# Blocks of 64 queries for the score maxima, and three elementwise jobs given to other engines

## The chip, the cores and the metric

One program runs on one core of a Trainium2 chip. The metric is device time in microseconds (us) of one execution; lower is better. The core's engines each work through their own instructions in order and meet through semaphores. They are called here as the profile calls them: TensorE is PE (its weight loads are PEld), VectorE is DVE, ScalarE is ACT, GpSimd is POOL, and SyncE is SP, whose work is to issue DMAs.

## The reference

Two results are computed from separate inputs and laid side by side. The first is causal attention with a sliding window; the second is a long convolution whose taps come from a state space model.

```python
# A: 2048 positions, width 576, 32 heads of 18, window 256
q, k, v = heads(x @ wqkv)
scores = einsum("bhqd,bhkd->bhqk", q, k) * 18 ** -0.5
mask = (i - j >= 0) & (i - j < 256)
p = softmax(where(mask, scores, -1e9))
a = concat_heads(p @ v) @ wo
# B: 2048 positions, 576 channels, 128 states
K = real(sum_n C * exp(dt * A * l) * dt * B)     # (576, 2048)
b = causal_conv(u, K) + u * Dskip                # by FFT of length 4096
out = concatenate([a, b], axis=-1)
```

All inputs and the output are fp32. The kernel keeps that accuracy where it uses 16 bit operands by splitting a number into a high and a low fp16 part.

## The kernel before, in words

The first 470 us project x to q, k and v (stored to memory in fp16, with a high and a low part) and build the taps of the convolution. Two transform steps of the convolution then run (the second, `s1_k`, ends near 515 us; its matmuls are L465 and its evacuations L132 on ScalarE and L134 on VectorE). After that comes the stage to which the change belongs, `attention`, from about 515 us to the end. Its order is written out by hand: what each engine's queue holds, and in which order, is what these loops issue.

**Units and items.** Attention is cut into 16 units: eight groups of four heads, for each half of the 2048 queries. A unit has 1024 queries of four heads, and six items (two chunks of 512 queries, three banks of key blocks each). For item n of 96 the loop interleaves several generators by their progress (`merge` always steps the one that is least advanced; of equals the first in the list). In list order they are: the scores of item n; a share of `gmax` for a later unit; the values of item n-2; a share of the convolution `conv`; and late in the loop parts of the output projection `wo_first` and `wo_part`.

- `scores` has two halves. Each issues the score matmuls (L676) into one of two buffers `ST`, then one exponential on ScalarE (L678, 128 x 1024), which writes `P`. At the end the masks of the diagonal blocks run on GpSimd (L687).
- `values` multiplies `P` by the values of the heads (L699); after a chunk ScalarE copies the sum out (L707).
- `gmax` finds for each query the largest score in its window, which is what the exponential subtracts. It runs one to three units ahead. Its unit begins at the fourth item (k = 3), right after the unit before it has been transposed and closed (L648, L650), so that its first step is issued behind the first half of that item's scores. The step copies q of the four heads into `qb`, a block diagonal operand, with two instructions on VectorE (L632, one for each half of the partitions). Then come 32 steps, one for a block of 32 queries: two matmuls (L640) of 64 columns each (two heads x 32 queries), stacked in one PSUM tile of the pool `ring`, and one fused add-and-maximum over 288 keys on VectorE (L643, followed in the trace by a read of its accumulator). The additive bias hides keys outside of the window. There is one `qb`; the pool `ring` has three buffers, which `conv`, `norm` and the output projection use too.
- `conv` runs in frequency space: matmuls L504, copies X on ScalarE (L527), products on VectorE (L530, L531, L534, L535), differences and sums on GpSimd (L539, L540), the inverse L511 with its copies on ScalarE (L512). From about 1000 us its last part runs in 16 rounds: load h (SP queue, L555) and u (GpSimd's queue, L559), multiply u by Dskip on GpSimd (L573), a matmul (L577), an add on VectorE (L579), and four stores through the SP queue (L123 is the helper that issues postponed DMAs).
- `norm` scales a finished unit: L735, L738 and L748 on VectorE, the high part of the quotient on ScalarE (L749), the low part on VectorE (L751), the matmul that spreads the denominators (L747), and four stores on GpSimd's queue (L755).

The maxima come back as a row of the operand `Q` through four small DMAs of the SP queue (`Q<-m`, issued by L123 one item after the transpose).

Of the kernel before, what the change touches and what calls it, by code (L numbers as in the profile page):

```python
# [10 lines left out]
F32 = mybir.dt.float32  # L11
F16 = mybir.dt.float16
BF = mybir.dt.bfloat16
I32 = mybir.dt.int32
AF = mybir.ActivationFunctionType
OP = mybir.AluOpType
# [22 lines left out]
def constants():  # L39
    c = {}  # L40
    tau = 2 * np.pi
    l1, l2, f1, f2 = np.arange(32), np.arange(64), np.arange(32), np.arange(64)
    ph = -tau * np.outer(l1, f1 + 0.25) / 32
    w1 = np.zeros((128, 2, 128))
    for s in range(4):
        w1[s * 32:s * 32 + 32, 0, s * 32:s * 32 + 32] = np.cos(ph)
        w1[s * 32:s * 32 + 32, 1, s * 32:s * 32 + 32] = np.sin(ph)
    w2 = np.zeros((128, 32, 128))
    i1 = np.zeros((128, 32, 128))
    for f in range(32):  # L50
        ph = -tau * np.outer(l2, f + 0.25 + 32 * f2) / 2048
        co, si = np.cos(ph), np.sin(ph)
        w2[0:64, f, 0:64], w2[64:128, f, 0:64] = co, -si
        w2[0:64, f, 64:128], w2[64:128, f, 64:128] = si, co
        i1[0:64, f, 0:64], i1[64:128, f, 0:64] = co.T, si.T
        i1[0:64, f, 64:128], i1[64:128, f, 64:128] = -si.T, co.T
    ph = tau * np.outer(f1 + 0.25, l1) / 32
    i2 = np.zeros((128, 64))
    for p in range(2):
        i2[p * 64:p * 64 + 32, p * 32:p * 32 + 32] = np.cos(ph) / 2048  # L60
        i2[p * 64 + 32:p * 64 + 64, p * 32:p * 32 + 32] = -np.sin(ph) / 2048
    mult = {"c_cm": np.arange(64), "c_ct": np.arange(32) + 0.5, "c_ca": np.r_[64 * np.arange(8), 512 * np.arange(4)],
            "c_cp": np.r_[np.zeros(8), np.full(4, 31.5)]}
    for nm, v in mult.items():
        t = np.zeros((3, GC, GC, len(v)))
        for g in range(GC):
            t[:, g, g] = v
        c[nm] = t.reshape(96, GC, len(v))
    bias = np.zeros((128, 2, 32))
    for p in range(128):  # L70
        bias[p, 0, :p % 32 + 1] = -1e30
        bias[p, 1, p % 32 + 1:] = -1e30
    c["c_w1"], c["c_w2"], c["c_i1"], c["c_i2"] = w1, w2, i1, i2
    c["c_id"], c["c_bias"] = np.eye(128), bias
    row = np.zeros((32, 32))
    row[18] = 1.0
    c["c_heads"] = np.concatenate([np.kron(np.eye(4), np.ones((32, 32))), np.tile(np.eye(32), (4, 1)),
                                   np.kron(np.eye(4), row)], axis=1)
    return {k: np.ascontiguousarray(v.astype(ml_dtypes.bfloat16 if k in mult else np.float32)) for k, v in c.items()}
# [27 lines left out]
class Kernel:  # L107
# [376 lines left out]
    def conv(self):  # L484
        nc, a, tt = self.nc, self.a, self.nc.vector.tensor_tensor
        fs, fy = self.p["fs"], self.p["fy"]

        def load(fp):
            t = {}
            for nm, src in (("w2", a["c_w2"]), ("i1", a["c_i1"])):  # L490
                t[nm] = fs.tile([128, 2, 128], F32, name=nm)
                nc.sync.dma_start(t[nm], src[:, 2 * fp:2 * fp + 2])
            for nm, g in (("tx", self.gx), ("tk", self.gk)):
                t[nm] = fs.tile([128, 4, 2, 144], F32, name=nm)
                nc.sync.dma_start(t[nm], g.rearrange("a l (s f) j -> (a l) s f j", s=4)[:, :, 2 * fp:2 * fp + 2, :])
            return t
# [20 lines left out]
        nx = load(0)  # L517
        last = None
        for fp in range(16):
            cu = nx  # L520
            ho = fs.tile([128, 2, D], F32, name="ho")
            for hs in range(2):
# [22 lines left out]
                if hs == 0 and fp < 15:  # L545
                    nx = load(fp + 1)
# [17 lines left out]
        nx = [loadh(0), loadh(1)]  # L564
        for _ in range(5):
            yield
        for qd in range(16):
            if qd < 14:
                nx.append(loadh(qd + 2))
            hp, ut = nx[qd]  # L570
            y = fy.tile([128, D], F32, name="t2")
            for e in range(qd + (qd > 0), min(qd + 2, 16)):
                nc.gpsimd.tensor_tensor(nx[e][1], nx[e][1], self.dsk, op=OP.mult)  # L573
            for hf in range(2):
                ps = ring()
                for k in range(2):
                    nc.tensor.matmul(ps[64 * k:64 * k + 64], self.i2, hp[:, k, hf * 288:hf * 288 + 288],  # L577
                                     start=True, stop=True)
                tt(y[:, hf * 288:hf * 288 + 288], ps, ut[:, hf * 288:hf * 288 + 288], op=OP.add)  # L579
                yield  # L580
            for k in range(4):
                self.after(1, nc.sync.dma_start, outv[4 * qd + k], y[32 * k:32 * k + 32])


    def att_setup(self):
        nc, a, ap = self.nc, self.a, self.p["att"]
        self.ident = ap.tile([128, 128], F32, name="ident")
        nc.sync.dma_start(self.ident, a["c_id"])
        self.bias = ap.tile([128, 288], F32, name="bias")
        nc.vector.memset(self.bias, 0.0)  # L590
        for e in range(2):
            nc.sync.dma_start(self.bias[:, 256 * e:256 * e + 32], a["c_bias"][:, e])
        self.qb = ap.tile([128, 2, 32, 64], F16, name="qb")
        nc.gpsimd.memset(self.qb, 0.0)
        self.sets = []
        for b in range(3):
            d = {"Q": ap.tile([128, 2, HQ], F16, name="Q%d" % b), "K": ap.tile([128, 2, HK], F16, name="K%d" % b)}
            nc.vector.memset(d["Q"], 0.0)
            for h in (0, 64):
                nc.vector.memset(d["K"][h:h + 32], 0.0)  # L600
                nc.vector.memset(d["K"][h + 32:h + 64], -32768.0)
            self.sets.append(d)
        self.od = self.p["dram"].tile([2, D, L], F16, name="od")
        hd = ap.tile([128, 288], F32, name="heads")
        nc.sync.dma_start(hd, a["c_heads"])
        self.same, self.pick, self.sums = hd[:, 0:128], hd[:, 128:160], hd[:, 160:288]
# [20 lines left out]
    def gmax(self, i):  # L627

        nc, (hf, g), d = self.nc, divmod(i, 8), self.sets[i % 3]
        m = self.p["m"].tile([128, 32], F32, name="m")  # L630
        for u in range(2):
            nc.vector.tensor_copy(self.qb[64 * u:64 * u + 54, :, :, 32 * u:32 * u + 32],  # L632
                                  d["Q"][64 * u:64 * u + 54].rearrange("p b (t q) -> p b t q", q=32))
        yield
        for t in range(32):
            ps = self.p["ring"].tile([128, 512], F32, name="r")
            k0 = 32 * t if hf > 0 or t >= 8 else 256
            n = 32 * t + 288 - k0
            for b in range(2):
                nc.tensor.matmul(ps[64 * b:64 * b + 64, :n], self.qb[:, b, t, :], d["K"][:, b, k0:k0 + n],  # L640
                                 start=True, stop=True, skip_group_check=True)
            jk = self.p["m"].tile([128, 288], F32, name="jk")
            nc.vector.tensor_tensor_reduce(out=jk[:, :n], in0=ps[:, :n], in1=self.bias[:, 288 - n:], scale=1.0,  # L643
                                           scalar=-3e38, op0=OP.add, op1=OP.max, accum_out=m[:, t:t + 1])
            yield
        yield
        mt = self.p["ring"].tile([128, 512], F32, name="r")
        nc.tensor.transpose(mt[:32, :128], m, self.ident)  # L648
        m16 = self.p["m"].tile([32, 128], F16, name="m16")
        nc.vector.tensor_scalar(m16, mt[:32, :128], 2.0 ** -15, None, op0=OP.mult)  # L650
        for j in range(4):
            r = 64 * (j % 2) + 54
            self.after(1, nc.sync.dma_start, d["Q"][r:r + 1, j // 2].rearrange("o (s q) -> o s q", q=32),
                       m16[:, 32 * j:32 * j + 32])
        yield

    BL = [(0, 0, 0, 1), (128, 2, 0, 3), (512, 1, 0, 2), (768, 4, 2, 4), (1024, 3, 1, 4), (1408, 5, 3, 4)]
# [66 lines left out]
    def norm(self, i):  # L724
# [3 lines left out]
        osb = self.osb.pop(i)  # L728
# [11 lines left out]
        if i == 7:  # L740
            h = self.h7[0] = self.p["h7"].tile([128, 2, HQ], F16, name="h7")
        else:
            h = np_.tile([128, 2, HQ], F16, name="oh16")
        for c in range(2):
            cs = slice(c * 512, c * 512 + 512)
            ps = self.p["ring"].tile([128, 512], F32, name="r")
            nc.tensor.matmul(ps, self.same, X[:, 16 * c:16 * c + 16].rearrange("p s q -> p (s q)"), start=True, stop=True)  # L747
            nc.vector.tensor_tensor(osb[:, cs], osb[:, cs], ps, op=OP.mult)  # L748
            nc.scalar.activation(h[:, 0, cs], osb[:, cs], AF.Copy)  # L749
            yield  # L750
            nc.vector.tensor_tensor(h[:, 1, cs], osb[:, cs], h[:, 0, cs], op=OP.subtract)  # L751
        yield
        for j in range(4 if i != 7 else 0):
            f0 = 72 * g + 18 * j
# [258 lines left out]
```

## Time and profile before

| what | us |
|---|---|
| median of 3 runs (lowest, highest) | 1142.4 (1141.99, 1145.32) |
| the profiled execution | 1142.89 |
| its span in the trace | 1141.2 |
| busy: PE, DVE, ACT, POOL | 921.1, 717.9, 624.2, 519.8 |
| mean granted TensorE clock | 0.925 of full speed |

A row of groups reads: line, engine, operation, output <- inputs, shapes, count | busy us, mean ns of one | idle time of that engine just before them, and what ended most of it. A timeline row reads: start, duration, engine, line, operation, tiles, shape, count, and in brackets the idle time before it with what ended it. A row of windows reads: the stretch, its length, then busy us and count for PE, PEld, DVE, ACT and POOL, then the granted TensorE clock, the busy share of the DMA engines and GB/s.

### The profile page before, as it was taken

The page shows a single profiled execution, that of the slowest core. Times are in us where ns is not written, and L with a number is a line of the kernel's source. Part 1 is how long each engine was busy: PE and PEld are TensorE (multiplying, and loading weights), DVE is VectorE, ACT ScalarE, POOL GpSimd, SP SyncE. Part 2 cuts the span into 40 slices and gives each one's busy share as a digit, 9 for nine tenths or more (in the row PEclk, how much of TensorE's full clock was granted, in tenths as well). Part 3 has the DMA queues.
Part 4 walks back from the last instruction along what each step waited for, and adds up shares of the span by engine and source line. Part 5 has one row for each costly group of instructions (what it writes and reads, how often), then busy time and mean ns, then how long its engine had stood idle before and what let it go on. Part 6 is the DMA issues. An engine that isn't in the chain of part 4 may idle for free.

```text
span 1141.2 us, 27005 instructions
## 1 busy us (share of the span) xinstructions
PE 921.1 (81%) x10412; PEld 450.9 (40%) x10412; DVE 717.9 (63%) x1805; ACT 624.2 (55%) x955; POOL 519.8 (46%) x618
## 2 busy tenths in 40 slices
PE   1535879887979789885888889889888999987876
PEld 0313436555545555532333333333333444433325
DVE  2879656866785562266667677787776566563344
ACT  1785778777878842231355555655555455544430
POOL 0014324442644330102355556666756555487860
PEclk9957989898989889998599998999999999999888
DMA  9564423433343325885153464544445334287753
GB/s 272 152 192 138 97 50 90 110 87 84 87 106 65 76 56 124 216 252 159 43 163 117 129 184 115 156 132 125 132 127 153 88 125 142 81 229 214 195 152 129
DMA packets 156186, 152.45 MB, mean 134 GB/s; under 512 B 37001, under 2 KB 134665, under 8 KB 155865
## 3 DMA queue, kind: packets, MB, share of 16 engines
q1 hardware_dynamic: 148488, 132.14, 42.3%
q0 software_dynamic: 6064, 14.60, 4.9%
q10 hardware_dynamic: 1504, 3.99, 1.3%
q8 instruction: 82, 1.34, 0.5%
q14 instruction: 48, 0.39, 0.1%
HBM read 89.27 MB, written 61.01 MB: 132 GB/s over the span
## 4 chain that ended last, share of the span: by engine, by line
PE 50%; DVE 19%; DMA 10%; ACT 9%; issue 7%; SPq 4%; POOL 1%; DVEq 0%; ACTq 0%; POOLq 0%
PE pp L176 8%; PE po L699 7%; PE r L504 6%; PE r L640 6%; PE r L893 4%; PE r L511 4%; PE ST L676 3%; PE pp L465 3%; PE kp L422 3%; PE r L747 3%; PE x L318 2%; DMA gk<-g 2%; DVE tr L362 2%; DMA K<-in_wqkv_dram 2%; DVE jk L643 1%
## 5 line engine op out<-in xcount | busy, mean ns | idle before, releaser
L643 DVE CUSTOM_DVE_ANT_0 jk<-r,bias 128x288 f32<-128x288 f32 (+7 forms) x512 | 206.5, 435 | 121.6 <-PE r L640 118.8
L678 ACT ACTIVATE P<-ST,esc 128x1024 f32<-128x1024 f32 (+1 forms) x192 | 203.3, 1059 | 93.9 <-PE ST L676 89.4
L384 POOL TENSOR_TENSOR m<-A,tr 128x1024 f32<-128x1024 f32 x72 | 149.6, 2099 | 194.1 <-PE kp L422 141.1
L687 POOL TENSOR_SCALAR_AFFINE_SELECT P<-P 128x512 f32<-128x512 f32 x240 | 158.1, 688 | 107.2 <-ACT P L678 105.0
L640 PE MATMUL r<-K,qb 128*64 128x288 f16 (+7 forms) x1024 | 134.9, 301 | 24.6 <-DVE t L531 5.9
L539 POOL TENSOR_TENSOR Y<-t,t 64x288 f32<-64x288 f32 x64 | 54.4, 849 | 149.8 <-DVE t L534 147.9
L699 PE MATMUL po<-P,V 128*32 128x256 f32 (+2 forms) x1408 | 118.8, 410 | 4.3 <-ACT osb L707 2.2
L640 PEld LDWEIGHTS <-qb 128*64 128x64 f16 x1024 | 61.0, 112 | 128.4 <-issue 78.6
L422 PE MATMUL kp<-Q,m 128*32 128x64 f32 x4608 | 87.9, 230 | 27.7 <-DVE Q L405 10.6
L422 PEld LDWEIGHTS kp<-Q,m 128*32 128x32 f32 x4608 | 75.0, 116 | 56.0 <-issue 40.4
L465 PE MATMUL pp<-ut,w 128*128 128x288 f32 x128 | 52.4, 535 | 42.8 <-DMA ut<-in_u_dram 25.8
L676 PE MATMUL ST<-Q,K 64*128 64x384 f16 (+2 forms) x704 | 75.8, 286 | 2.2 <-DMA Q<-m 2.1
L241 DVE SCALAR_TENSOR_TENSOR qst<-pp,qst 128x512 f16<-128x512 f32 x36 | 24.7, 686 | 64.2 <-ACT qst L240 64.1
L749 ACT ACTIVATE oh<-osb 128x512 f16<-128x512 f32 x28 | 17.6, 630 | 78.9 <-DVE osb L748 78.9
L132 ACT ACTIVATE g<-pp 128x288 f32<-128x288 f32 (+1 forms) x84 | 34.5, 447 | 39.7 <-DMA gk<-g 19.9
L504 PE MATMUL r<-tx,w 128*64 128x288 f32 x256 | 47.0, 448 | 10.8 <-DMA tx<-gx 9.2
L540 POOL TENSOR_TENSOR Y<-t,t 64x288 f32<-64x288 f32 x64 | 53.2, 831 | 3.8
L465 PEld LDWEIGHTS pp<-ut,w 128*128 128x128 f32 x128 | 28.8, 244 | 63.4 <-issue 26.4
L511 PE MATMUL r<-Y,i 128*128 128x288 f32 x128 | 50.7, 480 | 3.7 <-DVE m L643 1.5
L330 ACT ACTIVATE ab<-k 128x512 f32<-128x512 f32 (+1 forms) x54 | 31.9, 591 | 36.5 <-DVE k L329 36.0
L176 PE MATMUL pp<-xh,wh 128*128 128x512 f16 x180 | 47.8, 387 | 1.2 <-DVE xh L233 1.2
L504 PE MATMUL r<-tk,w 128*64 128x288 f32 x256 | 46.4, 443 | 2.8 <-DVE m L643 1.0
(176 smaller groups left out, 1814.3 us busy)
## 6 DMA issues: line engine op xcount, KB each, us to landing
gx<-g SPq DMA_DIRECT2D x32, 288.0 KB
qd<-qst SPq DMA_DIRECT2D x72, 128.0 KB
gk<-g SPq DMA_DIRECT2D x16, 576.0 KB
tx<-gx SPq DMA_DIRECT2D x16, 576.0 KB
tk<-gk SPq DMA_DIRECT2D x16, 576.0 KB
h<-ho SPq DMA_DIRECT2D x16, 576.0 KB
raw<-in_xT_dram SPq DMA_DIRECT2D x16, 512.0 KB
Q<-qd SPq DMA_DIRECT2D x32, 216.0 KB
```

The source lines that it names most:

```text
L176: self.nc.tensor.matmul(ps, u, v, start=(i == 0), stop=(i == len(ops) - 1))
L384: self.nc.gpsimd.tensor_tensor(m, A[:, ch, a0:a0 + 8].unsqueeze(3).to_broadcast(sh), tr[:, ch, part, 0:8].unsqueeze(2).to_broadcast(sh), o ...
L422: nc.tensor.matmul(kp[32 * st:32 * st + 32, c % 2 * JJ2 + j, :], m[:, ch, a0:a0 + 32], Q[:, ch, term % 2, :], start=(term == 0), stop=(ter ...
L465: nc.tensor.matmul(ps, self.w1[:, part, :], src[:, o:o + k], start=True, stop=True)
L504: nc.tensor.matmul(ps[64 * par:64 * par + 64], w2[:, par, 64 * part:64 * part + 64], t[:, 2 * hs:2 * hs + 2, par, :], start=True, stop=True)
L511: nc.tensor.matmul(ps, i1[:, par, :], Y[par], start=True, stop=True)
L640: nc.tensor.matmul(ps[64 * b:64 * b + 64, :n], self.qb[:, b, t, :], d["K"][:, b, k0:k0 + n], start=True, stop=True, skip_group_check=True)
L643: nc.vector.tensor_tensor_reduce(out=jk[:, :n], in0=ps[:, :n], in1=self.bias[:, 288 - n:], scale=1.0, scalar=-3e38, op0=OP.add, op1=OP.max ...
L676: nc.tensor.matmul(ps[:, u, o:o + n], d["K"][h, jp, k0:k0 + 128], d["Q"][h, jp, q0:q0 + n], start=True, stop=True, skip_group_check=True)
L678: nc.scalar.activation(pt[:, 2 * jp:2 * jp + 2, lo:hi], ps[:, :, lo:hi], AF.Exp, scale=self.esc)
L687: nc.gpsimd.affine_select(v, v, pattern=[[0, 4], [sg, 128]], compare_op=OP.is_ge, fill=0.0, base=-1 if far else 0, channel_multiplier=-sg)
L699: nc.tensor.matmul(self.po[32 * j:32 * j + 32, t0 * 128:t1 * 128], V[:, kb * 76 + 19 * j:kb * 76 + 19 * j + 32], pt[:, j, o:o + (t1 - t0) ...
```

## The change

Four things change, all in the attention stage.

1. `gmax` takes 64 queries a step. The operand `qb` holds 16 blocks of 128 columns (two heads x 64 queries) for each of the two head pairs b. A step is one matmul of 128 columns for one b against 320 keys, so there are 16 x 2 = 32 steps a unit as before, each with one matmul where there were two. The add-and-maximum covers 320 columns where it covered 288. The bias is one 128 x 320 constant that is loaded whole. The maxima lie in another order, and the four DMAs that bring them back read 16 partitions of 64 elements each, where they read 32 of 32.
2. The two copies into `qb` are issued on ScalarE, at the same place of the program.
3. The low part of the quotients in `norm` is computed on GpSimd.
4. u times Dskip is computed on VectorE.

```diff
-    bias = np.zeros((128, 2, 32))
+    bias = np.zeros((128, 320))
     for p in range(128):
-        bias[p, 0, :p % 32 + 1] = -1e30
-        bias[p, 1, p % 32 + 1:] = -1e30
+        bias[p, :p % 64 + 1] = -1e30
+        bias[p, 256 + p % 64 + 1:] = -1e30
...
             for e in range(qd + (qd > 0), min(qd + 2, 16)):
-                nc.gpsimd.tensor_tensor(nx[e][1], nx[e][1], self.dsk, op=OP.mult)
+                tt(nx[e][1], nx[e][1], self.dsk, op=OP.mult)
...
-        self.bias = ap.tile([128, 288], F32, name="bias")
-        nc.vector.memset(self.bias, 0.0)
-        for e in range(2):
-            nc.sync.dma_start(self.bias[:, 256 * e:256 * e + 32], a["c_bias"][:, e])
-        self.qb = ap.tile([128, 2, 32, 64], F16, name="qb")
+        self.bias = ap.tile([128, 320], F32, name="bias")
+        nc.sync.dma_start(self.bias, a["c_bias"])
+        self.qb = ap.tile([128, 2, 16, 128], F16, name="qb")
...
         for u in range(2):
-            nc.vector.tensor_copy(self.qb[64 * u:64 * u + 54, :, :, 32 * u:32 * u + 32],
-                                  d["Q"][64 * u:64 * u + 54].rearrange("p b (t q) -> p b t q", q=32))
+            nc.scalar.activation(self.qb[64 * u:64 * u + 54, :, :, 64 * u:64 * u + 64],
+                                 d["Q"][64 * u:64 * u + 54].rearrange("p b (t q) -> p b t q", q=64), AF.Copy)
         yield
-        for t in range(32):
-            ps = self.p["ring"].tile([128, 512], F32, name="r")
-            k0 = 32 * t if hf > 0 or t >= 8 else 256
-            n = 32 * t + 288 - k0
+        for t in range(16):
+            k0 = 64 * t if hf > 0 or t >= 4 else 256
+            n = 64 * t + 320 - k0
             for b in range(2):
-                nc.tensor.matmul(ps[64 * b:64 * b + 64, :n], self.qb[:, b, t, :], d["K"][:, b, k0:k0 + n],
-                                 start=True, stop=True, skip_group_check=True)
-            jk = self.p["m"].tile([128, 288], F32, name="jk")
-            nc.vector.tensor_tensor_reduce(out=jk[:, :n], in0=ps[:, :n], in1=self.bias[:, 288 - n:], scale=1.0,
-                                           scalar=-3e38, op0=OP.add, op1=OP.max, accum_out=m[:, t:t + 1])
-            yield
+                ps = self.p["ring"].tile([128, 512], F32, name="r")[:, :n]
+                nc.tensor.matmul(ps, self.qb[:, b, t, :], d["K"][:, b, k0:k0 + n], start=True, stop=True)
+                jk = self.p["m"].tile([128, 320], F32, name="jk")
+                o = 16 * b + t
+                nc.vector.tensor_tensor_reduce(out=jk[:, :n], in0=ps, in1=self.bias[:, 320 - n:], scale=1.0,
+                                               scalar=-3e38, op0=OP.add, op1=OP.max, accum_out=m[:, o:o + 1])
+                yield
...
-            self.after(1, nc.sync.dma_start, d["Q"][r:r + 1, j // 2].rearrange("o (s q) -> o s q", q=32),
-                       m16[:, 32 * j:32 * j + 32])
+            self.after(1, nc.sync.dma_start, d["Q"][r:r + 1, j // 2].rearrange("o (s q) -> o s q", q=64),
+                       m16[j // 2 * 16:j // 2 * 16 + 16, j % 2 * 64:j % 2 * 64 + 64])
...
-            nc.vector.tensor_tensor(h[:, 1, cs], osb[:, cs], h[:, 0, cs], op=OP.subtract)
+            nc.gpsimd.tensor_tensor(h[:, 1, cs], osb[:, cs], h[:, 0, cs], op=OP.subtract)
```

## The prediction, made before the changed kernel ran

> **What bounds the kernel now.** I read the page's chain of work that ended last first, then windows by stage, then groups with their shapes, then the timeline of single units.
>
> ```profile
> PE 50%; DVE 19%; DMA 10%; ACT 9%; issue 7%; SPq 4%; POOL 1%; DVEq 0%; ACTq 0%; POOLq 0%
> ```
>
> ```profile
> 540.00:1020.00 480.00, 425.01 (x3639) 171.08 (x3638) 325.11 (x1198) 259.59 (x362) 283.51 (x417) 0.96 0.45 130
> 1020.00:1110.00 90.00, 73.48 (x591) 28.19 (x589) 35.15 (x80) 39.06 (x51) 69.84 (x104) 0.89 0.72 197
> ```
>
> The reader sees that in the 480 us where score maxima, scores, values and convolution run together TensorE is busy 89% (425.01 of 480), VectorE 68%, GpSimd 59%, ScalarE 54%. So TensorE's queue sets the pace there: work taken from VectorE pays only where TensorE waits for it, and a new stop of TensorE is paid nearly whole. In the 90 us after 1020 the picture is another: TensorE 82%, GpSimd 78%, and the DMA engines rise from 0.45 to 0.72.
>
> **The copies into qb** (change 2) carry most of the sum. The groups give the price on both engines:
>
> ```profile
> L632 DVE COPY qb<-Q 54x2048 f16<-54x2048 f16 x32 | 25.0, 781 | 0.5
> L264 ACT ACTIVATE al<-nA_re 96x2304 bf16<-96x2304 f32 x1 | 2.1, 2122 | 1.7 <-DVE nA_re L296 1.7
> L294 ACT ACTIVATE dt<-dt 128x576 f32<-128x576 f32 x1 | 0.7, 667 | 0.0
> L428 ACT ACTIVATE K<-kp 128x512 f32<-128x512 f32 x18 | 18.5, 1030 | 7.3 <-PE kp L422 7.3
> ```
>
> ScalarE's two plain rows differ by 1455 ns over 1728 elements: 0.842 ns an element. For 2048 elements that is 2122 - 256 x 0.842 = 1906 ns against VectorE's 781. Two copies take 3.81 us. The dear end is L428, which writes in single scattered elements: 1030 ns for 512, twice the plain price. The new copies write runs of 64, so I take the plain price. Now one unit in the timeline:
>
> ```profile
> 624.74 0.39 PE L676 MATMUL ST<-Q,K 64*128 64x128 f16 x4
> 625.05 1.82 DVE L632 COPY qb<-Q 54x2048 f16<-54x2048 f16 x2
> 625.06 0.64 PE L699 MATMUL po<-P,V 128*32 128x256 f32 x8
> 625.26 1.11 ACT L678 ACTIVATE P<-ST,esc 128x1024 f32<-128x1024 f32 x1 [0.95 <-PE ST L676]
> 625.63 0.71 PE L504 MATMUL r<-tk,w 128*64 128x288 f32 x4
> 626.93 0.25 PE L640 MATMUL r<-K,qb 128*64 128x32 f16 x4 [0.59 <-DVE qb L632]
> 627.11 0.39 PE L676 MATMUL ST<-Q,K 64*128 64x128 f16 x4
> 627.87 0.71 PE L504 MATMUL r<-tk,w 128*64 128x288 f32 x4 [0.37 <-DVE m L643]
> ```
>
> After the first half of the scores TensorE has one step of values (L699) and one of convolution (L504) before the first matmul that reads qb, at 626.93, where it already waits 0.59 us for the copies on VectorE. On VectorE these start beside the exponential. On ScalarE, by the program's order, they stand behind it: it ends at 626.37, the copies at 626.37 + 3.81 = 630.18, and with some 0.06 us to wake TensorE (626.93 less the copies' end at 626.87) the matmul starts at 630.24, which is 3.3 us later. Behind it in TensorE's queue stand the second half of the scores (627.11), for which ScalarE's next exponential waits, and everything else: nothing covers the stop. The first and last of the fourteen units that start at a fourth item:
>
> ```profile
> 564.14 1.11 ACT L678 ACTIVATE P<-ST,esc 128x1024 f32<-128x1024 f32 x1 [3.46 <-PE ST L676]
> 566.25 0.32 PE L640 MATMUL r<-K,qb 128*64 128x32 f16 x4 [0.43 <-DVE qb L632]
> ...
> 1001.58 1.12 ACT L678 ACTIVATE P<-ST,esc 128x1024 f32<-128x1024 f32 x1 [2.08 <-PE ST L676]
> 1003.89 0.44 PE L640 MATMUL r<-K,qb 128*64 128x288 f16 x4
> ```
>
> The same sum gives 2.9 us (565.25 + 3.87 - 566.25) and 2.7 us. The fourteen are 2.9, 3.4, 3.3, 3.7, 2.9, 3.4, 3.7, 3.4, 3.7, 3.7, 2.1, 2.0, 2.0, 2.7: 43 us. The smaller ones at the end have 15 matmuls of the output projection ahead of the block matmul. The unit at item 0 adds 1.0. Gross **+44**. Some comes back, because VectorE is no longer behind when TensorE resumes: bracketed waits such as the 0.37 us at 627.87 add up to about 4 us in the 5 us after the first block matmul of these units: **-4** (0 at least; at most -15, one us a unit).
>
> At the very start ScalarE's first copy stands, in the changed order, before three evacuations of the convolution's last transform:
>
> ```profile
> 478.42 0.43 SPq L620 DMA_DIRECT2D Q<-qd  x1
> 479.98 1.32 ACT L132 ACTIVATE g<-pp 128x384 f32<-128x384 f32 x3 [1.08 <-DMA gk<-g]
> ```
>
> ```profile
> X<-in_u_dram POOLq DMA_DIRECT2D x32, 72.0 KB, 4.2
> ```
>
> A load of u from GpSimd's queue lands 4.2 us after its issue; by that, q is there at 482.5, the copy ends at 484.4, and those evacuations start 4.4 us late. The bracket shows that stage waiting for its stores, so I take **+4** (0 to +6, with the second copy).
>
> **The clock after a stop.** TensorE's granted clock halves after a stretch in which it worked little. Around the unit above:
>
> ```profile
> 622.76:626.17 3.41, 2.85 (x31) 1.12 (x27) 2.60 (x9) 2.46 (x4) 2.10 (x3) 1.00 0.82 271
> 626.17:629.59 3.42, 1.97 (x24) 0.99 (x22) 2.75 (x12) 1.78 (x3) 3.00 (x6) 1.00 1.00 325
> 629.59:633.00 3.41, 3.41 (x18) 1.00 (x20) 0.74 (x7) 1.06 (x2) 3.16 (x5) 0.50 0.12 34
> ```
>
> A stretch with 1.97 us of work in 3.42 (58%) was followed by 3.41 us at half speed, while one with 2.85 was not. A stop of some 3.5 us leaves 1.7 us idle in one of two neighbouring stretches at the least, so nearly every unit will now pay. A half-speed stretch does 1.7 us of full-speed work instead of about 2.9 (85% of 3.41), so it loses 1.2, and with 1.3 stretches a stop 1.5 us. Fourteen stops, most of them hit, give 20; less some 5 us that such stretches cost near copies already: **+15** (0 to +30). The Trainium skill, "TensorE: Matmul & The Clock Gate", Part 1, has the clock fall to half after an idle window of about 3.4 us and rise after a busy one; this trace agrees on the length and on the half, and differs in that 58% of work did not save the clock. By the page's idle window alone this term would be near 0 and the sum 15 us lower.
>
> **The block matmuls** (change 1). L640 goes from 1024 to 512 matmuls, but the two of a step ran side by side:
>
> ```profile
> 993.92 0.29 PE L893 MATMUL r<-woh,h 128*128 128x288 f16 x1
> 994.05 0.28 PE L893 MATMUL r<-wol,h 128*128 128x288 f16 x1
> 994.17 0.28 PE L893 MATMUL r<-woh,h 128*128 128x288 f16 x1
> 994.38 0.44 PE L640 MATMUL r<-K,qb 128*64 128x288 f16 x4
> 994.75 0.39 PE L676 MATMUL ST<-Q,K 64*128 64x256 f16 x4
> ```
>
> Full-width matmuls of 288 columns start 0.12 us apart. Two steps of L640 (four matmuls) take 0.37 us until the next group starts, 0.12 for each and 0.1 for a change of tile shape, which also shows at 994.17 to 994.38 (0.21 where the same shape takes 0.12). So a step costs about 0.123 us now and 0.123 x 320/288 = 0.137 then: 512 x 0.014 = +7 us. Shape changes are lost beside the convolution's L504 (same 128*64 shape now) and saved beside L511, L747 and L893 (128*128); between 540 and 1020 us these are 150 and 114 neighbours, so +3. With TensorE at 89%: **+8** (0 to +15).
>
> **The maxima on VectorE.**
>
> ```profile
> L643 DVE CUSTOM_DVE_ANT_0 jk<-r,bias 128x288 f32<-128x288 f32 x448 | 188.6, 453 | 98.0 <-PE r L640 95.7
> L643 DVE CUSTOM_DVE_ANT_0 jk<-r,bias 128x256 f32<-128x256 f32 x8 | 3.4, 422 | 0.5 <-PE po L699 0.2 <-PE r L640 0.2
> L751 DVE TENSOR_TENSOR oh<-osb,oh 128x512 f16<-128x512 f32 x28 | 23.7, 846 | 0.0
> L573 POOL TENSOR_TENSOR X<-X,dsk 128x576 f32<-128x576 f32 x8 | 11.3, 1413 | 1.0 <-DMA X<-in_u_dram 0.8
> L539 POOL TENSOR_TENSOR Y<-t,t 64x288 f32<-64x288 f32 x64 | 54.4, 849 | 149.8 <-DVE t L534 147.9
> ```
>
> 32 columns more cost 31 ns: 512 x 31 = 16 us of busy time, but VectorE waits 96 us for these matmuls, so most lies in its idle time: **+1** (0 to +16). **The low parts** (change 3): VectorE loses L751, 24 us and 2 us of its other form; it runs ahead of maxima that hand back a ring buffer: **-3** (0 to -15). On GpSimd one costs, between 849 ns for 288 and 1413 for 576 columns, 849 + 224 x 1.96 = 1288 ns: 30 make 39 us, in an engine 59% busy whose masks and differences are needed one step or two items later: **+1** (0 to +5). What hides it is GpSimd's idle 41%; without that it would cost the 39.
>
> **u times D** (change 4) and the last stage. GpSimd loses 16 x 1.413 = 22.6 us there and gains some 7 of low parts. VectorE gains 16 x 0.95 = 15 us (846 ns scaled from 512 to 576 columns), in an engine busy 39% of that stage, though the product for the next round now waits in VectorE's queue for u to land, with adds and the remaining maxima behind it.
>
> ```profile
> PE r L747 <- DVE spread L738: 6.5, 1, 6.5
> DVE t L579 <- DMA out_dram<-t: 20.7, 4, 11.7
> DVE t L579 <- DMA t<-in_u_dram: 6.4, 2, 5.3
> ```
>
> Among the waits between 1000 and 1110 us the store of y's buffer is the long one, which the change leaves as it is, so I take **-3** (-15, all that GpSimd sheds, to +15, all that VectorE gains). The four DMAs that return the maxima (L123, x4 at the transpose's heels) fall into the new stop and land earlier for the scores that need them:
>
> ```profile
> 790.57 5.27 DMA Q<-m
> 1007.88 6.07 DMA Q<-m
> ```
>
> These two waits stand in the chain; 3 us each at most, **-3** (0 to -6). The bias load and the memset that goes are under 1 us: 0.
>
> **The sum:** 44 - 4 + 4 + 15 + 8 + 1 - 3 + 1 - 3 - 3 = +60. The profiled execution took 1142.89 (its span 1141.2 and 1.7 around it), 0.5 above the median of the runs shown, 1142.4. So 1142.4 + 60 = **1202 us**.
>
> **Rivals.** (a) The stop is as told, but the clock holds and VectorE's relief gives more back: without the clock's 15 and with 10 more back, 1177. For it: between 540 and 1020 the clock averages 0.96. Against: the 626.17 window. (b) ScalarE's copies cost L428's price, 1.66 ns an element over the same 181 ns fixed (667 - 576 x 0.842), so 3.58 us each: 15 units x 3.3 more, 1252. Against: L428's scattered single elements. (c) Faster: VectorE, not TensorE, paces the loop through the ring of three buffers, so that all it sheds is gained: 25 of copies and 26 of low parts, less 16 and 15, gives -20, 1122. It decides from the point where ScalarE has finished the copies by the time TensorE has run out of other work, 1.9 us after the first scores in the unit at 624.7; the copies take twice that. Against it too: VectorE sat idle 98 us before L643, waiting for TensorE. (d) Fewer matmuls do save time, because the pairs in truth ran one after another: 512 x 0.123 = 63 us less, 1139. Against: four of them in 0.37 us. (e) Each stop holds the clock down for two stretches more: 14 x 2.4 = 34 more, 1236.
>
> **How the numbers follow.** The forecast 0.52, (a) 0.22, (b) 0.08, (c) 0.08, (d) 0.04, (e) 0.06. The range 1165 to 1232 takes in the first two with the bounds of clock, relief and matmuls, and leaves out the rest. Faster by over 0.3% (3.4 us, about what a measurement tells from no change): (c) and half of (d), 0.10; the same 0.02; slower 0.88.
>
> **What the changed profile would show.** L640 waiting 2 to 4 us for ScalarE's qb once a unit, ScalarE's copies at 1.9 us; half-speed windows after most of them; L640's busy time near 70 us; L643 at 484 ns; GpSimd's low parts at 1.3 us; less GpSimd busy after 1020. The prediction is wrong if ScalarE's copies end before TensorE needs them, if the maxima's matmuls take much less of TensorE, or if the last stage shrinks by tens of us.

## The result, and the profile after

The changed kernel takes **1214.47 us** (median; 1212.33 to 1216.53) against 1142.2 for the kernel before on the same chip: a ratio of **1.064 [1.061, 1.067]**, 72 us slower. The forecast was 1202 in a range of 1165 to 1232. The profiled execution took 1212.54 us, its span 1210.8, with TensorE's granted clock at 0.904 on average (0.925 before).

The page's chain of work that ended last, by engine:

```profile
PE 49%; DVE 17%; ACT 14%; DMA 11%; issue 5%; SPq 2%; POOL 1%; DVEq 0%; ACTq 0%; POOLq 0%
```

ScalarE's share went from 9% to 14%, and 4% of the span, some 48 us, is the one line of the copies. The page's groups for the lines that the change touches (L638 and L641 are L640 and L643 of before; L630 was L632, L749 was L751):

```profile
L641 DVE CUSTOM_DVE_ANT_0 jk<-r,bias 128x320 f32<-128x320 f32 (+4 forms) x512 | 221.8, 466 | 200.9 <-PE r L638 199.0
L638 PE MATMUL r<-K,qb 128*128 128x320 f16 (+4 forms) x512 | 138.7, 316 | 67.2 <-ACT qb L630 47.0
L630 ACT ACTIVATE qb<-Q 54x2048 f16<-54x2048 f16 x32 | 60.9, 1902 | 2.0 <-DVE g L134 1.5
```

TensorE stands idle 67.2 us before the maxima's matmuls, and 47.0 of it ends with ScalarE's copy. VectorE lost work, and now waits 200.9 us, nearly all of it for these matmuls, where it waited 121.6. One unit in the timeline of after, which answers to the unit at 624.74 of before (rows of other work between these are left out, here and in the timelines below):

```profile
638.41 0.39 PE L674 MATMUL ST<-Q,K 64*128 64x128 f16 x4
638.92 1.11 ACT L676 ACTIVATE P<-ST,esc 128x1024 f32<-128x1024 f32 x1 [1.11 <-PE ST L674]
639.30 0.71 PE L504 MATMUL r<-tk,w 128*64 128x288 f32 x4
639.93 3.83 ACT L630 ACTIVATE qb<-Q 54x2048 f16<-54x2048 f16 x2
643.82 0.29 PE L638 MATMUL r<-K,qb 128*128 128x64 f16 x2 [3.81 <-ACT qb L630]
644.04 0.61 PE L674 MATMUL ST<-Q,K 64*128 64x128 f16 x4
```

TensorE's last other work starts at 639.30 and ends at 640.01, ScalarE is through its exponential just then, and the two copies run for 3.83 us with TensorE idle for 3.81 of them. The stop comes between two halves of the scores, as the prediction had it. Windows of one length of the clock's records, over the same unit:

```profile
639.00:642.41 3.41, 1.00 (x12) 0.20 (x4) 0.82 (x2) 3.39 (x3) 2.75 (x5) 1.00 1.06 349
642.41:645.82 3.41, 2.00 (x12) 0.65 (x12) 0.38 (x4) 2.46 (x2) 0.00 (x0) 0.50 0.23 64
645.82:649.23 3.41, 3.35 (x17) 1.14 (x18) 1.61 (x8) 1.11 (x1) 2.66 (x4) 0.50 0.00 0
649.23:652.65 3.42, 3.22 (x34) 1.36 (x32) 2.24 (x11) 2.78 (x5) 3.35 (x6) 1.00 0.00 0
```

A stretch with 1.00 us of TensorE work is followed by one at half speed. That one still holds part of the stop (2.00 of 3.41 busy), so the next is at half speed too; only after a full one does the clock come back. The windows of the stage as a whole:

```profile
540.00:1020.00 480.00, 393.01 (x2740) 134.87 (x2738) 266.46 (x1024) 278.07 (x349) 254.22 (x375) 0.90 0.39 114
515.00:1063.00 548.00, 446.31 (x3098) 156.13 (x3099) 301.99 (x1167) 305.50 (x386) 284.53 (x421) 0.90 0.38 113
1063.00:1180.00 117.00, 94.06 (x713) 35.26 (x711) 55.28 (x129) 52.51 (x65) 70.15 (x124) 0.88 0.67 187
```

In the same 480 us TensorE is busy 82% (393.01) where it was 89%, at a clock of 0.90 where it was 0.96. From 515 us to the last unit's copies it takes 548 us where it took 486 (515 to 1001): 62 of the 70 us between the two spans. The rest to the end is 147 where it was 140, with one more stop in it.

### The profile page after: what moved, and what is told of

Same layout as the page of the kernel before. It is cut to its first block, busy times and chain, and to the rows that moved or that the text cites. A ratio compares the mean times of both kernels' runs of the same rounds, so it can differ in the third digit from the quotient of the medians.

```text
span 1210.8 us, 25609 instructions
## 1 busy us (share of the span) xinstructions
PE 948.1 (78%) x9900; PEld 435.2 (36%) x9900; DVE 698.9 (58%) x1758; ACT 683.9 (56%) x987; POOL 513.9 (42%) x632
## 4 chain that ended last, share of the span: by engine, by line
PE 49%; DVE 17%; ACT 14%; DMA 11%; issue 5%; SPq 2%; POOL 1%; DVEq 0%; ACTq 0%; POOLq 0%
PE pp L176 7%; PE po L697 7%; PE r L504 6%; PE r L638 6%; PE r L891 4%; PE ST L674 4%; ACT qb L630 4%; PE r L511 3%; PE kp L422 3%; PE r L745 3%; PE pp L465 3%; DMA gk<-g 2%; DVE jk L641 2%; PE x L318 2%; DVE tr L362 2%
## 5 line engine op out<-in xcount | busy, mean ns | idle before, releaser
L641 DVE CUSTOM_DVE_ANT_0 jk<-r,bias 128x320 f32<-128x320 f32 (+4 forms) x512 | 221.8, 466 | 200.9 <-PE r L638 199.0
L685 POOL TENSOR_SCALAR_AFFINE_SELECT P<-P 128x512 f32<-128x512 f32 x240 | 146.1, 638 | 155.7 <-ACT P L676 153.8
L638 PE MATMUL r<-K,qb 128*128 128x320 f16 (+4 forms) x512 | 138.7, 316 | 67.2 <-ACT qb L630 47.0
L697 PE MATMUL po<-P,V 128*32 128x256 f32 (+2 forms) x1408 | 124.2, 426 | 4.0 <-ACT osb L705 1.4
L539 POOL TENSOR_TENSOR Y<-t,t 64x288 f32<-64x288 f32 x64 | 53.3, 832 | 167.3 <-DVE t L534 165.4
L638 PEld LDWEIGHTS <-qb 128*128 128x128 f16 x512 | 43.0, 100 | 177.2 <-issue 92.2
L674 PE MATMUL ST<-Q,K 64*128 64x384 f16 (+2 forms) x704 | 79.2, 298 | 3.0 <-DMA Q<-m 3.0
L630 ACT ACTIVATE qb<-Q 54x2048 f16<-54x2048 f16 x32 | 60.9, 1902 | 2.0 <-DVE g L134 1.5
L540 POOL TENSOR_TENSOR Y<-t,t 64x288 f32<-64x288 f32 x64 | 51.2, 800 | 3.8
L504 PE MATMUL r<-tk,w 128*64 128x288 f32 x256 | 49.4, 467 | 1.8 <-DVE t L531 0.7
```

What stands on the lines that cost most here:

```text
L504: nc.tensor.matmul(ps[64 * par:64 * par + 64], w2[:, par, 64 * part:64 * part + 64], t[:, 2 * hs:2 * hs + 2, par, :], start=True, stop=True)
L630: nc.scalar.activation(self.qb[64 * u:64 * u + 54, :, :, 64 * u:64 * u + 64], d["Q"][64 * u:64 * u + 54].rearrange("p b (t q) -> p b t q", ...
L638: nc.tensor.matmul(ps, self.qb[:, b, t, :], d["K"][:, b, k0:k0 + n], start=True, stop=True)
L641: nc.vector.tensor_tensor_reduce(out=jk[:, :n], in0=ps, in1=self.bias[:, 320 - n:], scale=1.0, scalar=-3e38, op0=OP.add, op1=OP.max, accum ...
L674: nc.tensor.matmul(ps[:, u, o:o + n], d["K"][h, jp, k0:k0 + 128], d["Q"][h, jp, q0:q0 + n], start=True, stop=True, skip_group_check=True)
L685: nc.gpsimd.affine_select(v, v, pattern=[[0, 4], [sg, 128]], compare_op=OP.is_ge, fill=0.0, base=-1 if far else 0, channel_multiplier=-sg)
```

## The experiments

Each is the kernel before or the kernel after with one edit. The ratio is to the kernel before on the same chip. "Half-speed time" is what the clock's records after 515 us show at half speed, in windows of 3.41 us of which several can follow each other: 80 us in the trace of before, 151 in that of after. Of the longer edits only the main lines are shown.

### Which part costs: the copies back, and the copies alone

The kernel after with its copies on VectorE again (`a_copies_dve`), and the kernel before with nothing changed but its copies put on ScalarE (`b_copies_act`):

```diff
-            nc.scalar.activation(self.qb[64 * u:64 * u + 54, :, :, 64 * u:64 * u + 64],
+            nc.vector.tensor_copy(self.qb[64 * u:64 * u + 54, :, :, 64 * u:64 * u + 64],
...
-            nc.vector.tensor_copy(self.qb[64 * u:64 * u + 54, :, :, 32 * u:32 * u + 32],
+            nc.scalar.activation(self.qb[64 * u:64 * u + 54, :, :, 32 * u:32 * u + 32],
```

> The changed kernel with one part undone: the two copies into qb are back on VectorE, everything else as changed. Theory S (the stop of TensorE for ScalarE's copies, and the half-speed stretches after it, are nearly the whole loss): 1142 to 1152 us, no wait of 2 us or more before the first block matmul of a unit, and half-speed time after 515 us back from 151 to about 80 us. Rival W (the wide blocks, the low parts on GpSimd or u times D on VectorE carry a good part): 1165 us or more.

> The kernel before with that part alone: its two copies into qb (blocks of 32) issued on ScalarE. Theory S: 1142 + 47 of stops + some 20 of clock, 1200 to 1214 us, with some 3.8 us idle on TensorE before the first block matmul of most units. Rival W: the loss needs the wide blocks too, 1175 us or less here.

With the copies back the time is 1145.0 us, **1.004 [1.002, 1.006]**; the copies alone give 1210.1 us, **1.058 [1.053, 1.063]**. Nearly all of the 6.4% is change 2, and the other three parts together cost 0.4%. The groups of the copies alone:

```profile
L640 PE MATMUL r<-K,qb 128*64 128x288 f16 (+7 forms) x1024 | 140.6, 313 | 69.7 <-ACT qb L632 49.7
L632 ACT ACTIVATE qb<-Q 54x2048 f16<-54x2048 f16 x32 | 60.9, 1902 | 1.1 <-DMA Q<-qd 0.8
```

and of the kernel after without them:

```profile
L638 PE MATMUL r<-K,qb 128*128 128x320 f16 (+4 forms) x512 | 135.3, 310 | 19.5 <-DVE t L531 4.2
```

The idle time before the maxima's matmuls comes and goes with the copies on ScalarE: 69.7 and 19.5 us. So does the half-speed time: 151 and 83.

### The stop against the clock: matmuls in the stop

In each unit but the first, 16 matmuls (8 in the last four units) that need only K are put ahead of the first block matmul, so that TensorE has work while ScalarE copies. Nothing reads what they write.

```diff
+                if t == 0 and b == 0 and i > 0:
+                    fill = self.p["ring"].tile([128, 512], F32, name="r")
+                    for _ in range(16 if i < 12 else 8):
+                        nc.tensor.matmul(fill, d["K"][:, 0, 256:384], d["K"][:, 0, 256:768], start=True, stop=True)
```

> The changed kernel with 16 matmuls that nothing reads (8 in the last four units) ahead of the first block matmul of each unit but the first, so that TensorE works while ScalarE copies; the wait for the copies stays. Theory S: the clock holds, half-speed time falls by 40 us or more and the time by about 20, to 1190 to 1202 us, though TensorE does more. Rival C (the half-speed stretches cost nothing, since TensorE catches up or waits anyway): 1212 us or more.

It measured 1191.3 us, **1.043 [1.040, 1.046]**: 23 us faster than the kernel after, by added work that is thrown away. One unit in its timeline, and the windows over it:

```profile
636.90 3.83 ACT L630 ACTIVATE qb<-Q 54x2048 f16<-54x2048 f16 x2
636.90 3.63 PE L640 MATMUL r<-K 128*128 128x512 f16 x16
...
640.78 0.23 PE L642 MATMUL r<-K,qb 128*128 128x64 f16 x2 [0.26 <-ACT qb L630]
```

```profile
635.61:639.02 3.41, 3.41 (x24) 1.35 (x23) 0.96 (x3) 3.11 (x3) 3.10 (x6) 1.00 1.09 387
639.02:642.43 3.41, 3.15 (x23) 1.14 (x21) 0.79 (x6) 2.76 (x2) 0.00 (x0) 1.00 0.40 88
642.43:645.84 3.41, 3.03 (x29) 1.28 (x28) 2.23 (x14) 2.25 (x4) 3.09 (x4) 1.00 0.00 0
```

The block matmul waits as long as it did (the copies still take 3.83 us), but the clock stays at 1.00, and the half-speed time falls from 151 to 74 us. So the clock is worth some 23 us; the intervals of the two times leave about 5 us either way, and in three units the added matmuls outlast the copies by 0.4 to 1.3 us, so that they cost a little themselves. What is left, 51 us over the kernel before (1139.9 beside this run), is the stop and the small parts.

### Half of the stop

The first copy on ScalarE, the second on VectorE, so that they run side by side (`dst` and `src` stand for the same slices as in the kernel after):

```diff
-            nc.scalar.activation(...)
+            if u == 0:
+                nc.scalar.activation(dst, src, AF.Copy)
+            else:
+                nc.vector.tensor_copy(dst, src)
```

> The changed kernel with one of the two copies on ScalarE and the other on VectorE. Theory S: the copy on ScalarE ends 1.9 us after the exponential, so the stop is about 1.5 to 1.9 us a unit instead of 3.8, too short in most units to bring the clock down: 1160 to 1180 us. Rival H (any wait for ScalarE brings the clock down): 1190 us or more.

It measured 1177.4 us, **1.032 [1.029, 1.035]**. Waits of this kernel from 540 to 1010 us (us in total, times, longest):

```profile
PE r L642 <- ACT qb L633: 19.0, 10, 2.8
```

Half of the copies on ScalarE cost about half of the whole (2.8% over the kernel with both on VectorE, against 6.0%), and the half-speed time stands between too, at 116 us. The time lies in the range of theory S, but its clause that these stops are too short for the clock missed. Each of the nine stops of 1.8 to 2.2 us, in the units from 600 to 885 us, has one or two windows at half speed behind it. The windows over one of them:

```profile
635.14:638.55 3.41, 1.53 (x16) 0.54 (x12) 1.40 (x8) 2.76 (x3) 2.05 (x4) 1.00 1.02 304
638.55:641.96 3.41, 3.25 (x17) 1.09 (x16) 1.57 (x8) 1.55 (x2) 2.72 (x4) 0.50 0.08 23
```

### ScalarE's idle time: six pieces early

ScalarE is idle for 46% of the stage before. If that time were free, the copies should vanish in it when they start early enough. Here `qb` is four tiles, and of the eight pieces of a unit six are copied one to two items before TensorE needs them. The edit is made to the kernel after (`a_early`) and, with blocks of 32, to the kernel before (`b_early`):

```diff
+                if k in (1, 2) and 0 < i < 14:
+                    streams.append((self.qcopies(i + 2, (0, 1) if k == 1 else (2,)), 6 - 2 * k))
```

> The changed kernel with the copies still on ScalarE but cut in eight pieces (qb as four tiles), six of them issued one and two items earlier, each behind an exponential, and the last two at the old place, where only the last steps of the unit read them. Theory S (what costs is the stop, not ScalarE's 61 us of work): the stop goes, 1140 to 1160 us. Rival B (ScalarE, busier by 60 us, delays the exponentials and TensorE with them): 1180 us or more.

> The kernel before (blocks of 32, low parts on VectorE, u times D on GpSimd) with its copies on ScalarE in eight early pieces. Theory S: VectorE's 25 us of copies and TensorE's wait for them (13 us on the chain of before) go, 1125 to 1140 us, faster than before. Rival B (ScalarE's added work delays the exponentials): 1150 us or more.

Both missed theory S and lie where rival B has them: 1182.0 us, **1.037 [1.034, 1.039]**, and 1170.4 us, **1.027 [1.024, 1.030]**. The waits for `qb` were gone almost wholly, but other waits came. Timeline of `a_early`, an item in which pieces are copied:

```profile
657.26 0.62 ACT L631 ACTIVATE qb<-Q 54x512 f16<-54x512 f16 x1
657.78 0.39 ACT L512 ACTIVATE ho<-r 128x288 f32<-128x288 f32 x1
658.19 0.63 ACT L631 ACTIVATE qb<-Q 54x512 f16<-54x512 f16 x1
658.73 0.45 PE L647 MATMUL r<-K,qb 128*128 128x320 f16 x2
658.85 0.69 ACT L685 ACTIVATE P<-ST,esc 128x512 f32<-128x512 f32 x1
...
659.43 0.62 ACT L631 ACTIVATE qb<-Q 54x512 f16<-54x512 f16 x1
...
660.37 0.63 ACT L631 ACTIVATE qb<-Q 54x512 f16<-54x512 f16 x1
661.00 0.60 ACT L714 ACTIVATE osb<-po 128x512 f32<-128x512 f32 x1
661.63 1.11 ACT L685 ACTIVATE P<-ST,esc 128x1024 f32<-128x1024 f32 x1
661.70 1.51 PE L706 MATMUL po<-P,V 128*32 128x384 f32 x8 [1.78 <-ACT osb L714]
```

Four pieces, 2.5 us together, stand in ScalarE's queue ahead of the copy of the values (L714), and the next values (L706) need the buffer that it empties. The profile's row for this wait, from 540 to 1010 us:

```profile
PE po L706 <- ACT osb L714: 9.8, 5, 2.5
```

In `b_early` the profile names GpSimd's masks (L696) for the longest such waits, but the copy of the values is again what came last:

```profile
895.03 0.62 ACT L633 ACTIVATE qb<-Q 54x512 f16<-54x512 f16 x1
895.20 1.22 POOL L696 TENSOR_SCALAR_AFFINE_SELECT P<-P 128x512 f32<-128x512 f32 x2 [3.86 <-ACT P L687]
...
895.97 0.63 ACT L633 ACTIVATE qb<-Q 54x512 f16<-54x512 f16 x1
896.61 0.60 ACT L716 ACTIVATE osb<-po 128x512 f32<-128x512 f32 x1
...
897.30 0.43 PE L708 MATMUL po<-P,V 128*32 128x128 f32 x8 [3.03 <-POOL P L696]
```

The masks end at 896.42, the copy at 897.21, and the values start 0.09 us later. Counted so, by values that start within 0.12 us of the end of this copy and whatever the profile names, TensorE's idle time before them is 20.6 us in `a_early` and 22.1 in `b_early`, against 1.9 in the trace of before. The half-speed time rose to 130 and 103 us, with 45 and 16 us more of TensorE work in it than before; half of that, 22 and 8 us, is an estimate of what the clock took. Together that is 41 and 28 us, about the 41 and 30 that were measured (`a_early` holds the other three parts as well, some 4 us); no run holds the clock up here to part the two. That ScalarE does its queue in order is also what the Trainium skill has ("TensorE: Matmul & The Clock Gate", Part 1, on queue depths: strict first in, first out, where TensorE may pull weight loads ahead); the trace agrees: in `a_early` the copy of the values starts at 661.00, just as the fourth piece ends.

### The same pieces, one behind each exponential

If place, and not the amount of work, is what costs, the same eight pieces should be nearly free when no more than one or two stand together. One quarter of `qb` is copied in each of items 2 to 5, for the unit two ahead:

```diff
+                if k >= 2 and i < 14:
+                    streams.append((self.qcopies(i + 2, (k - 2,)), 2))
```

> As the kernel with early copies on ScalarE (1182 us), but no more than one piece behind each exponential: the quarter r of qb is copied in item 2 + r of the unit, one to one and a half items before the block matmuls that read it, so that the copies of po into osb never stand behind more than one piece. Theory P (what was left of the loss there is the place in ScalarE's queue: pieces in a row ahead of the osb copy, for which values waited): 1145 to 1165 us, and no wait of values for osb over 1 us. Rival B (80 us more work on ScalarE, in whatever order, costs its share): 1175 us or more.

It measured 1149.2 us, **1.007 [1.005, 1.010]**, with more ScalarE work than in the kernel after. The group of its copies:

```profile
L631 ACT ACTIVATE qb<-Q 54x512 f16<-54x512 f16 x128 | 79.7, 623 | 3.0 <-DVE g L134 1.4
```

79.7 us against 60.9 of whole copies, yet 65 us less of time, so it isn't the amount of ScalarE's work that costs, as rival B had it. Its timeline shows a first block matmul that waits for nothing:

```profile
629.19 1.11 ACT L685 ACTIVATE P<-ST,esc 128x1024 f32<-128x1024 f32 x1 [0.34 <-PE ST L683]
630.20 0.62 ACT L631 ACTIVATE qb<-Q 54x512 f16<-54x512 f16 x1
630.80 1.11 ACT L685 ACTIVATE P<-ST,esc 128x1024 f32<-128x1024 f32 x1
```

```profile
630.20 0.23 PE L647 MATMUL r<-K,qb 128*128 128x64 f16 x2
```

The half-speed time is 76 us, as before the change. TensorE's idle time before the values, counted as above, fell to 7.1 us; two of these waits are just over 1 us (1.14 and 1.02), so that theory P's clause on them missed by a little. It isn't a gain either: against the kernel after with both copies on VectorE (1.004) the 25 us taken off VectorE bring nothing that can be seen.

### The small parts one by one

Blocks of 64 alone (`b_blocks64`: the kernel after with the copies, the low parts and u times D back where they were), the low parts on GpSimd alone (`b_low_ud`, which despite its name leaves u times D on GpSimd), and u times D on VectorE alone (`b_ud_dve`). The last two:

```diff
-            nc.vector.tensor_tensor(h[:, 1, cs], osb[:, cs], h[:, 0, cs], op=OP.subtract)
+            nc.gpsimd.tensor_tensor(h[:, 1, cs], osb[:, cs], h[:, 0, cs], op=OP.subtract)
...
-                nc.gpsimd.tensor_tensor(nx[e][1], nx[e][1], self.dsk, op=OP.mult)
+                tt(nx[e][1], nx[e][1], self.dsk, op=OP.mult)
```

> The kernel before with the blocks of 64 queries alone (copies, low parts and u times D stay where they were). Theory S: 512 matmuls of 0.137 us for 512 pairs of 0.123, and 31 ns more for each maximum, mostly hidden: 1144 to 1156 us. Rival F (half the matmuls and weight loads save TensorE time): 1135 us or less. Rival D (the longer maxima are paid in full): 1158 us or more.

> The kernel before with the low parts on GpSimd alone. Theory S: VectorE loses 26 us that were mostly hidden, GpSimd gains some 39 that are hidden too: 1135 to 1145 us. Rival G (GpSimd's masks and differences come late): 1148 us or more.

> The kernel before with u times D on VectorE alone. From the other parts (all but the copies +0.4%, wide blocks +0.1%, low parts -0.4%) this one should be +0.5 to +0.9%: 1146 to 1151 us. Rival T (GpSimd's relief in the last stage gains): 1140 us or less.

| alone | us | ratio |
|---|---|---|
| blocks of 64 | 1141.79 | 1.001 [0.999, 1.002] |
| low parts on GpSimd | 1135.29 | 0.996 [0.994, 0.998] |
| u times D on VectorE | 1142.32 | 1.001 [0.999, 1.003] |

The first and the third lie below the ranges of their theories S (1144 to 1156 and 1146 to 1151 us), the second at the lower end of its range. The kernel before with only the low parts moved is faster than both kernels. Its group:

```profile
L751 POOL TENSOR_TENSOR oh<-osb,oh 128x512 f16<-128x512 f32 x28 | 32.4, 1157 | 5.9 <-ACT oh L749 5.9
```

Blocks of 64 and u times D can't be told from no change. The three add up to -0.2%, the three together (`a_copies_dve`) measured +0.4%; the difference of 0.6% is more than the intervals together leave (about 0.4%), so the parts may not simply add; no run here settles it.

### An attempt at more: spread pieces on VectorE with the low parts on GpSimd

```diff
+                nc.vector.tensor_copy(self.qb[r][h, :, :, 32 * u:32 * u + 32],
+                       q[h].rearrange("p b (t q) -> p b t q", q=32)[:, :, 8 * r:8 * r + 8])
```

> The kernel before with its copies on VectorE spread in the same way (two pieces an item, ahead of their readers), and the low parts on GpSimd. Theory S: the wait for the copies goes (13 us of the chain before, of which VectorE's backlog keeps a part) and the low parts give 0.3% again: 1118 to 1134 us, faster than before. Rival N (VectorE only moves its delay to other places): 1135 us or more.

It missed: 1145.4 us, **1.003 [1.001, 1.006]**, and the low parts' gain is gone. The group of the pieces:

```profile
L633 DVE COPY qb<-Q 54x512 f16<-54x512 f16 x128 | 61.4, 479 | 2.0
```

A piece has a quarter of the elements and takes 479 ns on average where the whole took 781, so 61.4 us of VectorE replace 25.0. The average hides two kinds. The 51 pieces with no GpSimd work beside them take 271 to 292 ns. Those that start while a GpSimd instruction runs (74) mostly end some 0.15 us after that instruction does: the piece at 700.23 takes 884 ns, with GpSimd's L539 running for its first 0.74 us. The longest takes 5.0 us, beside a row of GpSimd instructions. At 0.287 us each the 128 pieces would be 37 us, so some 25 of the 61.4 are time beside GpSimd. That the longer time on VectorE is what took the gain back is likely, but wasn't tried by itself.

## Why the prediction was right, point by point

The direction and the mechanism held; the forecast was 12 us short, because terms were mis-sized in both directions. The stop and the clock together came out 16 us above their net forecast (48 and 23 against 40 and 15). That the block matmuls and the start of the stage were put too high hid a part of that, which is luck.

- **The stop.** Forecast 44 gross and 4 given back. TensorE's idle time right before the first block matmul of the 16 units was 3.1 us in total in the trace of before and is 50.8 now (4.7 in the unit at item 0, 3.7 to 3.8 in the next ten, 1.9 to 2.5 in the last four): **+48**. The fourteen units that start at a fourth item gained 43 us, as forecast; the one at item 0 gained 4.7 where 1.0 was reckoned. The price of a copy was right to 4 ns (1906 forecast, 1902 measured). Whether VectorE's relief gave back 4 us can't be told: what is left with the clock held up (`a_filler`) is 51 us, less some 4 for the small parts 47, beside a stop of 48, and the intervals leave some 4 us either way.
- **The clock.** The right mechanism with too small a size: forecast +15, measured 23 by the filled stop. The trace gives the same by another way: half-speed time rose by 71 us, with 52 us more of TensorE work done in it, and half of 52 is 26 us, an estimate. The mis-sized part of the term is the 1.3 stretches a stop. Ten of the stops have two windows at half speed from the stop on, because a 3.8 us stop reaches into a second window, as 2.00 us of work in 3.41 shows above. There are 21 windows more than before, where 15 us at 1.2 each are 12 or 13; the 1.2 us that one costs was about right (26 over 21).
- **The Trainium skill's rule on the clock** ("TensorE: Matmul & The Clock Gate", Part 1: half speed after an idle window of about 3.4 us) agrees on the length, and on the return after one busy window. Read as an idle window it would have made this term near 0. The runs show that it is a window with too little work: 1.00 us of 3.41 halves it, and 2.00 of 3.41 keeps it at half. Over the 13 traces after 515 us, a full-speed window with under 40% of TensorE work was followed by half speed in 66 of 66 cases, with 40 to 60% in 62 of 84, with 60 to 70% in 8 of 101, and with more in 1 of 1679. From half speed the clock came back after none of 129 windows with under 80% of work, and after 154 of 184 with 90% or more.
- **The start of the stage.** Forecast +4; it was 0. This step failed: the first copy ran at 478.84 us, not at 482.5, and the evacuations behind it started at 480.82, 0.8 us later than before and not 4.4. The second copy, at 487.13, delayed nothing that set the pace either, for the first block matmul started at 522.3 us where it had at 523.2.
- **The block matmuls.** Forecast +8; alone they measure +1 (-1 to +3). Two steps of after stand 0.38 us ahead of the next group, about as the forecast's price has it (twice 0.137 and 0.1 for the change of shape):

```profile
701.88 0.45 PE L638 MATMUL r<-K,qb 128*128 128x320 f16 x2
702.26 0.28 PE L674 MATMUL ST<-Q,K 64*128 64x256 f16 x2
```

  What failed is the comparison with before: there the same price gives 0.346 where the row shows 0.37. Taken over all places at full clock where two steps stand ahead of scores and nothing waits, the median is 368 ns before (64 places) and 377 after (59), 9 ns more and not 28; single steps ahead of values take 243 and 239. So some 2 us of the 7 were there. The sign for it, "L640's busy time near 70 us", was wrong too: it is 138.7, for that row counts the run of each matmul (316 ns), not the distance between starts (137 ns in the forecast).
- **The maxima** have the size forecast (487 ns against 484 for 320 columns) and cost nothing that can be seen, under VectorE's idle time before L641.
- **The low parts** cost GpSimd 1174 ns (1157 alone) where 1288 was forecast, and pay 0.4%, some 4 us, where -3 and +1 were taken.
- **u times D and the last stage.** Forecast -3; alone it is within the measurement of 0. GpSimd's busy time there fell as forecast (70.15 of 117 us after 1063, where it had 88 of 109 from 1001), and the time did not follow, so GpSimd did not bound that stage. On VectorE it took 14.8 us, as forecast (15), and VectorE waited 19.3 us for u to land before it; neither shows in the time.
- **The returned maxima** (`Q<-m`): the two waits of 5 and 6 us left the chain, as forecast; one of 1.99 at 544.77 is left, where before had one of 1.70 at 543.51.

By the rivals: that the clock holds (a) is refuted by `a_filler`, dear copies (b) by 1902 ns, VectorE as the bound (c) by `b_low_ud`, where 26 us less of VectorE gain 4 to 5, and pairs in series (d) by `b_blocks64`. Two stretches more a stop (e) had the right place but not the size: it is two in all in ten stops, not two more, and its 34 us stand against the 8 to 11 that the clock took beyond the forecast.

## What to carry to other kernels

An engine's idle share by itself is no room for work: ask what stands behind the moved work in its queue, and who waits for that. The copies on ScalarE, with the other three parts, cost 6.4% in one block ahead of TensorE's next work, 3.7% in pieces that stand ahead of a buffer's release, and 0.7% one behind each exponential. A stop of TensorE of 3.8 us was paid about one and a half times here, once as idle time and again as half speed after it, and stops of 1.9 us brought half speed too. Where a stop can't be avoided, matmuls whose result nobody reads bought a third of the loss back here.

## What the runs showed of the hardware that was not expected

- The clock asks for a share of work, not for a pause: a window of 3.41 us with 1.00 us of work halves it, one with 1.53 us does too, and 2.00 us of work at half speed don't bring it back. Throw-away matmuls in the stops made the kernel 23 us faster.
- On VectorE an fp16 copy of 512 elements took 271 to 292 ns with no GpSimd work beside it, and one that started while GpSimd was at work mostly ended some 0.15 us after GpSimd's instruction, and the longest took 5.0 us (`b_spread_dve_low`). On ScalarE the same copy took 623 ns on average, and one of 2048 elements 1902.
- A subtraction of 512 columns that took 846 ns on average on VectorE (681 at the least) took 1157 on GpSimd, only 1.4 to 1.7 times as long.
